# Sliding-window attention by key blocks, and projections of four tiles in two half passes

## The chip, the core and the metric

The kernel runs on one core of a Trainium2 chip. The core has five engines with their own instruction streams: PE (TensorE, matrix products into PSUM), DVE (VectorE), ACT (ScalarE), POOL (GpSimd) and SP (SyncE, which here issues DMAs). They wait for one another through semaphores. The metric is the device time of one execution in microseconds (us), as the median of several runs; a profiled execution gives the trace.

## The reference

Two layers of the same kind follow one another, with the same weights. Each adds an attention block and a block that changes a single row:

```python
def _A_ref(x, wqkv, wo):                      # S = 2048, D = 512
    H = 32; Dh = D // H; W = 256
    q, k, v = split(x @ wqkv)                 # 32 heads of 16
    scores = einsum("bhqd,bhkd->bhqk", q, k) * (Dh ** -0.5)
    mask = (i - j >= 0) & (i - j < W)
    p = softmax(where(mask, scores, -1e9))
    return einsum("bhqk,bhkd->bhqd", p, v) @ wo

def _B_ref(x, w_r, w_gate, w_up, w_down):     # F = 1792
    r = x @ w_r
    idx = argsort(-r)[:, :1]                  # the one row with the largest r
    y = (silu(x[idx] @ w_gate) * (x[idx] @ w_up)) @ w_down
    return x + scatter(y * sigmoid(r[idx]), idx)

x = A_x
x = x + _A_ref(layernorm(x)); x = x + _B_ref(layernorm(x))
x = x + _A_ref(layernorm(x)); x = x + _B_ref(layernorm(x))
```

Inputs and output are bf16.

## The kernel before

The 2,048 rows are 16 tiles of 128, so the two layers are 32 steps. The class Builder adds operations (engine, function, what it reads and writes, PSUM banks, an assumed duration, a priority) to a scheduler, Sched, which simulates them and fixes the order of each engine; a wait is put where an operand comes from another engine or a DMA. The priority is the step number plus a fraction, so that one step's work of several kinds is interleaved. Sched gives every engine a fixed order: an instruction that waits holds up all behind it.

**Projections** (proj, L546). The normalized tile XN (L521 on POOL, with 64 columns repeated at L523) is transposed by PE in sixteen half-height pieces (transposes, L525) into PSUM banks 6 and 7 (MISC), copied to XNT (evict_t, L544), and multiplied with the weights. The array is used as two row halves of 64, each with its own matmul and its own bank: in qk (L562) the upper half makes q and the lower k. For this the weights are stored split (load_split), and each half goes through all eight 64-row chunks; the repeated columns give each half the chunks that would lie in the other. The four column groups s (eight heads each) take 16 matmuls of 128 columns each, 64 for a tile. DVE copies k to KTN and q to QT (L569, L571). The v projection (L580) is 16 matmuls of 256 columns.

**Keys and values.** Keys are scattered into block-diagonal form, KBD, by eight DMAs on SP for a pair of tiles (kscat, L606); values go through DRAM (vd) into VBD (vscat, L616 and L622).

**Attention** (attention, L626). A step handles one query tile. For each of the four groups s there are three units (UNITS), which pack pieces of nine key blocks of 32 into 384 columns. A unit is up to eight score matmuls (L668), two matmuls that add the mask (L682), one exp on ACT over two banks (L689, 768 columns) into PT, and PV, 16 matmuls of 34 columns for every four blocks (L702). Units alternate between bank pairs 0/1 and 2/3; PV accumulates in banks 4 and 5. Then DVE takes the reciprocal of the denominators (L719) and normalizes (L724), and POOL repeats 64 columns (L726).

**Output projection** (out_proj, L728) transposes, multiplies (L742) and adds to the residual (L746), again in banks 6 and 7. mod_tile computes layernorm statistics and the router's value r on DVE and POOL.

**The one row.** After all 16 tiles of layer 0, select finds the row, through DRAM and gathers; mlp (L858) computes gate and up (L873, 56 matmuls each) and down (L888, 14) in bank 6, and later tiles get the row by a masked add (L509) from tile SKIP1 = 6 on, so the first six may be normalized before the row is known. In layer 1 the choice is made from NS2 = 13 tiles and its MLP is at the end of attention. If the row lies elsewhere, or a denominator is out of range, a flag starts a second, slower program (GBuilder) behind the first.

All of x lies in SBUF (XR, 16 tiles), and so do the three MLP weights, loaded once (L495 to L497). The steady order is set in build (L943): a step adds attention of tile T, output projection of T-1, and normalization and projection of T+3.

Of the kernel before, what the change touches and what calls it, by code (L numbers as in the profile page):

```python
# [8 lines left out]
F32 = mybir.dt.float32  # L9
BF16 = mybir.dt.bfloat16  # L10
I32 = mybir.dt.int32
ALU = mybir.AluOpType
# [44 lines left out]
class _Op:  # L57
    __slots__ = ("idx", "eng", "fn", "deps", "dur", "name", "is_dma", "prio", "signals", "count",
                 "dma_sem", "start", "end", "waits", "dma_extra")

    def __init__(self, idx, eng, fn, deps, dur, name, is_dma, prio):
# [14 lines left out]
        self.dma_extra = 0.0  # L76


class Sched:
# [64 lines left out]
    def needs_wait(self, op, dop):  # L144
        return dop.is_dma or dop.eng != op.eng or op.eng not in self.INORDER
# [175 lines left out]


UNITS = (
# [3 lines left out]
)  # L327
ACC = 4
MISC = 6
STEP = 1.0  # L330
NS2 = 13
SKIP1 = 6
DLO = 2.0 ** -60
DHI = 2.0 ** 60


class Builder:
# [16 lines left out]
    def alloc(self):  # L354
        nc = self.nc
        NT, SEQ, FF, NF = self.NT, self.SEQ, self.FF, self.NF
        self.RP = 3
        self.RQ = 6
        self.NU = 15
        self.XR = self.sb("XR", [128, NT, 516], F32)  # L360
        self.WQK = self.sb("WQK", [128, 8, 512], BF16)
        self.WV = self.sb("WV", [128, 8, 256], BF16)
        self.WO = self.sb("WO", [128, 8, 256], BF16)
        self.WG = self.sb("WG", [128, 4, FF], BF16)
        self.WU = self.sb("WU", [128, 4, FF], BF16)
        self.WD = self.sb("WD", [128, NF, 512], BF16)
        self.XN = self.sb("XN", [128, 2, 576], BF16)
        self.XNT = self.sb("XNT", [128, 2, 8, 128], BF16)
        self.QT = self.sb("QT", [128, self.RQ, 4, 128], BF16)
        self.KTN = self.sb("KTN", [128, 2, 2, 4, 128], BF16)  # L370
        self.KBD = self.sb("KBD", [128, self.RP, 2, 4, 4, 128], BF16)
        self.VN = self.sb("VN", [128, 2, 2, 4, 8, 17], BF16)
        self.VBD = self.sb("VBD", [128, self.RP, 8, 2, 8, 17], BF16)
        self.PT = self.sb("PT", [128, self.NU, 2, 512], BF16)
        self.ON = self.sb("ON", [128, 2, 576], BF16)
        self.OT = self.sb("OT", [128, 2, 8, 128], BF16)
        self.OUTB = self.sb("OUTB", [128, 2, 2, 512], BF16)
        self.JUNK = self.sb("JUNK", [128, 512], BF16)
        self.WR16 = self.sb("WR16", [128, 512], BF16)
        self.YBC = self.sb("YBC", [128, 512], F32)  # L380
        self.ONESB = self.sb("ONESB", [128, 128], BF16)
        self.ZEROB = self.sb("ZEROB", [128, 128], BF16)
# [40 lines left out]
    def xbf(self, m):  # L423
        return self.XR[:, m, 256:512].bitcast(BF16)

    def xin(self, L, m):
        return self.xbf(m) if L == 0 else self.XR[:, m, 0:512]
# [1544 lines left out]
```

## Time and profile before

| | us |
|---|---|
| median of 3 runs | 496.41 |
| lowest and highest | 495.53, 499.56 |
| profiled execution | 501.95 |
| its span, first to last instruction | 500.2 |

The profiled execution is 1.1% above the median. A row of the profile names the line, engine, operation, tile written and tiles read, and sizes. PEld is the loading of weights for a matmul. Slices are fortieths of the span. "issue" as the end of a wait means that nothing that the profile shows was waited for. A row of the stretches gives, for PE, PEld, DVE, ACT and POOL, the busy time and the number of instructions, then PE's granted clock and the DMA share and rate.

### The profile page before, as it was taken

What the parts mean: (1) busy time and instruction counts of PE and PEld (TensorE: products, weight loads), DVE (VectorE), ACT (ScalarE), POOL (GpSimd) and SP (SyncE); (2) the same over time, 40 slices, a digit from 0 to 9 for tenths busy, and PEclk for the clock granted to TensorE, in tenths of its full rate; (3) what the DMA queues carried; (4) which work ended last, traced back from release to release, by engine and by line L of the source; (5) the groups of instructions that cost most, each with busy time, mean ns of one, the idle gap of its engine ahead of it and who ended that gap; (6) DMA issues with size and microseconds to landing.
All of it is one profiled execution on the core that took longest, in us unless ns stands there. A gap on an engine that the chain in (4) does not pass through costs nothing.

```text
span 500.2 us, 29488 instructions
## 1 busy us (share of the span) xinstructions
PE 364.2 (73%) x13757; PEld 319.2 (64%) x13757; DVE 256.5 (51%) x558; ACT 274.4 (55%) x389; POOL 174.6 (35%) x438
## 2 busy tenths in 40 slices
PE   0168777887887787778787776777877787877860
PEld 0156767776776777777775654676776777766730
DVE  7663655555465554545567218765444555445242
ACT  0013467665676766666666620366666776787600
POOL 8721343233433443332324204644333332222012
PEclk9999999998999999999999567699999999998575
DMA  8982214131322222231323111232131404043000
GB/s 209 365 239 47 47 27 95 21 82 34 67 50 61 57 57 60 56 61 47 68 56 60 36 47 14 54 78 60 62 76 47 91 25 103 17 107 77 6 2 29
DMA packets 104808, 34.99 MB, mean 70 GB/s; under 512 B 87266, under 2 KB 100707, under 8 KB 104420
## 3 DMA queue, kind: packets, MB, share of 16 engines
q1 hardware_dynamic: 97428, 25.60, 22.4%
q10 hardware_dynamic: 7248, 7.41, 4.7%
q8 instruction: 110, 1.80, 1.5%
q14 instruction: 22, 0.18, 0.1%
HBM read 14.56 MB, written 14.22 MB: 58 GB/s over the span
## 4 chain that ended last, share of the span: by engine, by line
PE 57%; ACT 13%; issue 11%; DVE 8%; DMA 5%; ACTq 2%; POOL 1%; SPq 0%; DVEq 0%
ACT PT L689 13%; PE PS L562 12%; PE PS L668 12%; PE PS L702 12%; PE PS L742 6%; PE PS L580 6%; PE PS L536 3%; PE PS L682 2%; PE PS L888 2%; DMA WR<-in_B_w_r_dram 2%; ACTq L439 2%; DMA KBD<-KTN 1%; PE PS L873 1%; DVE VN L588 1%; DVE ON L724 1%
## 5 line engine op out<-in xcount | busy, mean ns | idle before, releaser
L689 ACT ACTIVATE PT<-PS 128x768 bf16<-128x768 f32 (+5 forms) x384 | 272.6, 772 | 164.7 <-PE PS L682 156.4
L668 PE MATMUL PS<-QT,KBD 64*128 64x128 bf16 (+3 forms) x2880 | 130.8, 208 | 41.3 <-ACT PT L689 26.8
L702 PE MATMUL PS<-VBD,PT 64*128 64x34 bf16 x5760 | 122.9, 176 | 23.5 <-issue 20.2
L702 PEld LDWEIGHTS PS<-VBD,PT 64*128 64x128 bf16 x5760 | 103.4, 94 | 29.4 <-issue 26.2
L668 PEld LDWEIGHTS PS<-QT,KBD 64*128 64x128 bf16 x2880 | 84.9, 96 | 57.5 <-ACT PT L689 36.9
L562 PE MATMUL PS<-XNT,WQK 64*128 64x128 bf16 x2048 | 73.7, 232 | 19.1 <-issue 9.8
L682 PE MATMUL PS<-BM,II 64*128 64x64 bf16 (+2 forms) x768 | 80.5, 200 | 1.2 <-issue 1.2
L562 PEld LDWEIGHTS PS<-XNT,WQK 64*128 64x128 bf16 x2048 | 66.6, 102 | 22.4 <-issue 17.3
L521 POOL TENSOR_SCALAR XN<-XR,RS 128x512 bf16<-128x512 bf16 (+1 forms) x32 | 24.5, 765 | 119.5 <-PE PS L536 106.9
L726 POOL COPY ON<-ON 128x64 bf16<-128x64 bf16 x32 | 7.9, 246 | 115.4 <-DVE ON L724 115.4
L569 DVE CAST KTN<-PS 128x512 bf16<-128x512 f32 x32 | 22.0, 688 | 47.2 <-PE PS L562 46.1
L746 DVE TENSOR_TENSOR XR<-PS,XR 128x512 f32<-128x512 f32 x32 | 22.1, 692 | 45.1 <-PE PS L742 43.8
L588 DVE CAST VN<-PS 128x512 bf16<-128x512 f32 x32 | 22.2, 693 | 39.7 <-PE PS L580 39.7
L682 PEld LDWEIGHTS PS<-BM,II 64*128 64x128 bf16 x768 | 42.0, 98 | 0.7 <-issue 0.7
L580 PE MATMUL PS<-WV,XNT 64*128 64x256 bf16 x512 | 36.8, 284 | 3.7 <-DVE QT L571 1.7
L742 PE MATMUL PS<-WO,OT 64*128 64x256 bf16 x512 | 35.9, 282 | 3.9 <-DVE OT L544 3.8
L544 DVE COPY OT<-PS 128x1024 bf16<-128x1024 bf16 x32 | 22.1, 689 | 27.4 <-PE PS L536 27.4
L536 PE MATMUL PS<-IDB,XN 64*128 64x64 bf16 x512 | 14.8, 196 | 24.1 <-POOL XN L523 17.2
L580 PEld LDWEIGHTS PS<-WV,XNT 64*128 64x128 bf16 x512 | 25.1, 99 | 7.6 <-DVE QT L571 2.6
L742 PEld LDWEIGHTS PS<-WO,OT 64*128 64x128 bf16 x512 | 24.5, 98 | 7.2 <-DVE OT L544 4.3
L536 PEld LDWEIGHTS PS<-IDB,XN 64*128 64x128 bf16 x512 | 10.4, 98 | 27.9 <-POOL XN L523 17.2
L724 DVE TENSOR_TENSOR ON<-PS,RD 128x256 bf16<-128x256 f32 x64 | 24.3, 418 | 0.8
(90 smaller groups left out, 363.3 us busy)
## 6 DMA issues: line engine op xcount, KB each, us to landing
scrx<-XR SPq DMA_DIRECT2D x14, 516.0 KB, 3.3
vd<-VN SPq DMA_DIRECT2D x15, 272.0 KB, 3.5
VBD<-vd SPq DMA_DIRECT2D x60, 68.0 KB, 2.5
KBD<-KTN SPq DMA_DIRECT2D x120, 32.0 KB, 3.2
XR<-in_A_x_dram SPq DMA_DIRECT2D x8, 256.0 KB, 8.9
WG<-in_B_w_gate_dram ACTq DMA_DIRECT2D x1, 1792.0 KB, 13.8
WU<-in_B_w_up_dram ACTq DMA_DIRECT2D x1, 1792.0 KB, 17.6
WD<-in_B_w_down_dram ACTq DMA_DIRECT2D x1, 1792.0 KB, 24.1
```

Of the source, the lines that this page charges most:

```text
L521: S.add("pool", lambda e: e.tensor_scalar(out=XN[:, k2, 0:512], in0=x, scalar1=RS[:, k4, 1:2], scalar2=RS[:, k4, 2:3], op0=ALU.mult, op1=A ...
L536: r = e.transpose(o, src[rows, idx, c:c + 128], self.IDB[rows, rows])
L544: S.add("dve", lambda e: e.tensor_copy(out=out, in_=src), banks=[MISC, MISC + 1], writes=[key], dur=620, name=name)
L562: r = e.matmul(self.PS[:, MISC + t, 128 * s:128 * s + 128], lhsT=self.WQK[rows, j, 128 * s:128 * s + 128], rhs=XNT[rows, k2, j, :], start= ...
L580: r = e.matmul(o, lhsT=XNT[rows, k2, j, :], rhs=self.WV[rows, j, :], start=(j == 0), stop=(j == 7))
L588: S.add("dve", lambda e: e.tensor_copy(out=vout, in_=vin), banks=[MISC, MISC + 1], writes=["vn%d_%d" % (pr % 2, m % 2)], dur=600, name="evv")
L668: r = e.matmul(self.PS[:, pair + x, c0:c0 + n], lhsT=self.KBD[rows, p3, tt, s, b4, :], rhs=self.QT[rows, q, s, q0:q0 + n], start=(bi == 0) ...
L682: r = e.matmul(o, lhsT=self.II[rows, :], rhs=w, start=False, stop=True, skip_group_check=True)
L689: return e.activation(out=self.PT[:, slot, :, off:off + ncols], in_=self.PS[:, pair:pair + 2, 0:ncols], func=ACTF.Exp, scale=0.25)
L702: r = e.matmul(acc[:, x, 34 * gg:34 * gg + 34], lhsT=self.PT[rows, slot, a, c:c + 128], rhs=self.VBD[rows, p3, 4 * tt + b4, :, gg, :], sta ...
L724: S.add("dve", lambda e, o=o, i0=i0, i1=i1: e.tensor_tensor(out=o, in0=i0, in1=i1, op=ALU.mult), reads=["rd%d_%d" % (L, t)], banks=[ACC + ...
L742: r = e.matmul(self.PS[:, MISC + x, 0:256], lhsT=self.OT[rows, k2, j, :], rhs=self.WO[rows, j, :], start=(j == 0), stop=(j == 7))
```

## The change

**Projections of four tiles.** Four tiles are normalized and transposed into one XNT of 512 columns (NBATCH = 4). The weights are stored plainly (WQKV), and eight transposes a tile are left. A projection has two passes: in the first the upper row half makes q (bank 6) and the lower k (bank 7), in the second they change places, so each output gets both halves of every 128-row chunk. The first matmul of the second pass waits until the first pass has been written (`force`, a wait of PE for itself). The v and the output projection are built alike. Matmuls of qk have 512 columns: 64 for four tiles.

**Key-major attention.** A step handles the four key blocks of one tile. Each block is scored for the 288 queries that can see it in one matmul a row half, masked at both ends by another, and exponentiated over 2 x 288 columns. PT keeps twelve key blocks, with zeroed edges, and the PV of query tile T takes the blocks of tiles T-2, T-1 and T, in three parts per group.

**Rest.** XR holds 12 tiles; layer 1 reads x back from DRAM (SCR). MLP weights come in six chunks of 896 KB on SP, through two buffers, in each layer (in layer 1 two chunks use the space of WQKV and XNT). Layer 0 chooses its row from NS1 = 11 tiles, its MLP is spread over the steps behind, and the row is corrected in DRAM before it is read back; the row must lie in tile 8 or later (SKIP1), and no later tile may have a larger value (late). In layer 1 NS2 is 12. The first batch scatters its keys on DVE, straight from PSUM, and is normalized on ACT; KBD has two buffers instead of three. The wrapped copies on POOL and the masked add are gone.

```diff
-NS2 = 13
-SKIP1 = 6
+NBATCH = 4
+NS1 = 11
+NS2 = 12
+SKIP1 = 8
+W = 288
+PITCH = 384
...
     def needs_wait(self, op, dop):
+        if op.force == dop.idx:
+            return True
...
-            for j in range(8):
-                c = 128 * j if j < 4 else 128 * (j - 4) + 64
+            for j in range(4):
                 for t in range(2):
...
+    def phases(self, fn, reads, dur, at, name, parts=1, gap=0.03, bank=MISC):
+        S = self.S
+        last = None
+        n = 4 // parts
+        for ph in range(2):
+            for k in range(parts):
+                js = range(n * k, n * k + n)
+                i = S.add("pe", lambda e, ph=ph, js=js: fn(e, ph, js), reads=reads, banks=[bank, bank + 1], dur=dur / parts, name=name,
+                          prio=at + gap * (parts * ph + k), extra_deps=[last] if last is not None else [])
+                if ph == 1 and k == 0:
+                    S.ops[i].force = last
+                last = i
+
+    def qk(self, b, s, at):
...
+        bank = (MISC, 0, 2, ACC)[s] if b == 0 else MISC
...
-                    r = e.matmul(self.PS[:, MISC + t, 128 * s:128 * s + 128], lhsT=self.WQK[rows, j, 128 * s:128 * s + 128],
-                                 rhs=XNT[rows, k2, j, :], start=(j == 0), stop=(j == 7))
+                    w = t ^ ph
+                    r = e.matmul(self.PS[:, bank + w, :], lhsT=self.WQKV[rows, j, 512 * w + 128 * s:512 * w + 128 * s + 128],
+                                 rhs=XNT[rows, kb, j, :], start=(ph == 0 and j == 0), stop=(ph == 1 and j == 3), skip_group_check=True)
...
         for s in range(4):
-            for u in range(3):
...
+            for b in range(4):
+                kb = 4 * t + b
+                n = min(W, self.SEQ - 32 * kb)
+                q0 = 32 * kb
...
+                        r = e.matmul(self.PS[:, pair + x, 0:n], lhsT=self.KBD[rows, k2, s, 4 * (T % 2) + b, :],
+                                     rhs=self.QT[rows, s, q0:q0 + n], start=True, stop=False, skip_group_check=True)
...
+                    o = self.PT[:, c0 - 96:c0 - 96 + 2 * PITCH].rearrange("p (a c) -> p a c", a=2)[:, :, 96:96 + n]
+                    return e.activation(out=o, in_=self.PS[:, pair:pair + 2, 0:n], func=ACTF.Exp, scale=0.25)
...
+            for part, (r0, r1) in enumerate(((-8, -4), (-4, 0), (0, 4))):
+                blocks = [4 * t + r for r in range(r0, r1) if 4 * t + r >= 0]
...
-            if T == NT + 1:
-                self.select(0, NT, at + 0.3)
...
-            g = T + 3
-            if g < NW:
-                lnp(g, at)
-                prj(g, at)
...
+            for L, n in ((0, NS1), (1, NS2)):
+                u = T - L * NT - n
+                if u == -2:
+                    self.load_mlp(0, at)
+                    self.load_mlp(1, at)
+                elif u == 0:
+                    self.select(L, n, at + 0.3)
+                elif u == 2:
+                    self.mlp_in(L, at - 0.6)
...
+                elif u == (5 if L == 0 else 4):
+                    self.mlp_down(L, 0, at - 0.4)
+                    self.mlp_down(L, 1, at - 0.2)
...
+            misc(T, at)
```

The order of PE in a steady step before, around the q/k projection of a tile. L668 and L682 are a score unit, L702 is PV, L562 the projection:

```order
L702 MATMUL PS<-VBD,PT 128x34 x16
L562 MATMUL PS<-XNT,WQK 128x128 x64
L668 MATMUL PS<-QT,KBD 128x64 x2
L668 MATMUL PS<-QT,KBD 128x128 x4
L668 MATMUL PS<-QT,KBD 128x64 x2
L682 MATMUL PS<-BM,II 128x2x2x32 x2
L668 MATMUL PS<-QT,KBD 128x96 x2
```

The order of PE in a steady step of the changed kernel, around the q/k projection of one group of four tiles (L584), its second pass behind the first; L682 and L688 are a score block, L716 is PV:

```order
L716 MATMUL PS<-VBD,PT 128x34 x32
L584 MATMUL PS<-XNT,WQKV 128x512 x8
L682 MATMUL PS<-QT,KBD 128x288 x2
L688 MATMUL PS<-BM,II 128x2x32 x2
L584 MATMUL PS<-XNT,WQKV 128x512 x8
L682 MATMUL PS<-QT,KBD 128x288 x2
L688 MATMUL PS<-BM,II 128x2x32 x2
L682 MATMUL PS<-QT,KBD 128x288 x2
L688 MATMUL PS<-BM,II 128x2x32 x2
L716 MATMUL PS<-VBD,PT 128x34 x48
```

64 matmuls in one run have become two runs of eight, with a score block of four matmuls between them.

The order of PE at the layer boundary before. XST is the chosen row, WG, WU and WD the MLP weights; L536 with L562 and L580 are projections of layer 1, L742 the output projection:

```order
L702 MATMUL PS<-VBD,PT 128x34 x16
L873 MATMUL PS<-XST,WG 128x1 x56
L873 MATMUL PS<-XST,WU 128x1 x56
L702 MATMUL PS<-VBD,PT 128x34 x32
L888 MATMUL PS<-WD,HT 128x512 x14
L536 MATMUL PS<-IDB,XN 128x64 x16
L562 MATMUL PS<-XNT,WQK 128x128 x64
L580 MATMUL PS<-WV,XNT 128x4x64 x16
L536 MATMUL PS<-IDB,ON 128x64 x16
L742 MATMUL PS<-WO,OT 128x256 x16
```

The order of PE around the first half of the gate and up products (L916, weights in MW) of layer 0 in the changed kernel, in tile 14:

```order
L682 MATMUL PS<-QT,KBD 128x256 x2
L688 MATMUL PS<-BM,II 128x32 x2
L716 MATMUL PS<-VBD,PT 128x34 x16
L916 MATMUL PS<-XST,MW 128x1 x56
L682 MATMUL PS<-QT,KBD 128x224 x2
L688 MATMUL PS<-BM,II 128x32 x2
L716 MATMUL PS<-VBD,PT 128x34 x16
L584 MATMUL PS<-XNT,WQKV 128x512 x8
L682 MATMUL PS<-QT,KBD 128x192 x2
```

The MLP products now stand among score blocks of layer 0, and the projections of layer 1 no longer stand behind them.

The order of PE at the end, before (L937 is the flag):

```order
L702 MATMUL PS<-VBD,PT 128x34 x48
L888 MATMUL PS<-WD,HT 128x512 x14
L536 MATMUL PS<-IDB,ON 128x64 x16
L742 MATMUL PS<-WO,OT 128x256 x16
L536 MATMUL PS<-IDB,ON 128x64 x16
L742 MATMUL PS<-WO,OT 128x256 x16
L937 MATMUL PS<-ONESB,BADB 1x1
```

And in the changed kernel (L954 is the down product, L1006 the flag):

```order
L716 MATMUL PS<-VBD,PT 128x34 x64
L546 MATMUL PS<-IDB,ON 128x64 x8
L750 MATMUL PS<-WO,OT 128x256 x16
L954 MATMUL PS<-MW,HT 1x512 x14
L1006 MATMUL PS<-ONESB,BADB 1x1
```

One output projection is left behind the last PV instead of two, and the down product has moved from ahead of it to behind it.

More of the change, by code (lines that the diff above doesn't have):

```diff
@@ L658, in loc @@
[L658 to L669 removed]
+                fr = (4 * s + b) / 16.0
@@ L707, in pv @@
[L707 to L716 removed]
+                                r = e.matmul(self.PS[:, ACC + x, 34 * gg:34 * gg + 34], lhsT=self.PT[rows, c:c + 128],
+                                             rhs=self.VBD[rows, v3, b8, :, gg, :], start=st, stop=last and kb == blocks[-1] and a == 1,
+                                             skip_group_check=True)
@@ L787, in mod_tile @@
[L787 to L800 removed]
+              reads=[sk], writes=[rk], dur=260)
```

754 lines of the change are left out of this document (404 added, 350 removed), and 3 rows, old and new, of the table UNITS.

## The prediction

> **What bounds the kernel now.** I read the page first, then the start times of one instruction that comes once per query tile, then the stretches, and last the waits of the matrix engine. In the page's busy table and slices, PE is the busiest engine at 73%, and ACT falls to nothing at three places: the first three slices, slices 25 and 26, and the last two.
>
> ```profile
> span 500.2 us, 29488 instructions
> PE 364.2 (73%) x13757; PEld 319.2 (64%) x13757; DVE 256.5 (51%) x558; ACT 274.4 (55%) x389; POOL 174.6 (35%) x438
> PE   0168777887887787778787776777877787877860
> ACT  0013467665676766666666620366666776787600
> q8 instruction: 110, 1.80, 1.5%
> ```
>
> The reciprocal of the denominators (L719) runs once at the end of each tile's attention, so its starts are the pace. The rows are the whole run, a stretch in the first layer, one in the second, and the pair around the layer boundary.
>
> ```profile
> L719 DVE RECIPROCAL RD<-PS x32: 347/353/358, 49.1 to 476.0; 128x32 f32<-128x32 f32 x32
> L719 DVE RECIPROCAL RD<-PS x11: 348/357/358, 120.0 to 249.2; 128x32 f32<-128x32 f32 x11
> L719 DVE RECIPROCAL RD<-PS x8: 347/348/358, 348.1 to 439.9; 128x32 f32<-128x32 f32 x8
> L719 DVE RECIPROCAL RD<-PS x2: 348/353/358, 294.8 to 334.6; 128x32 f32<-128x32 f32 x2
> ```
>
> So the span has four parts: 49.1 us until the first tile is done; a steady step of (249.2-120.0)/10 = 12.9 and (439.9-348.1)/7 = 13.1 us, 13.0 in all; one pair of tiles 39.8 us apart at the boundary; and 500.2-476.0 = 24.2 us behind the last tile.
>
> Within the steady step, PE is busy 15.66 of 20 us, which is 10.2 of 13.0, and ACT 14.41 of 20. What PE does in the rest is in the second and third row: each stretch holds exactly 128 weight loads and 128 matmuls, and begins behind a stop of PE for which nothing is waited for.
>
> ```profile
> 180.00:200.00 20.00, 15.66 (x668) 14.30 (x670) 9.47 (x19) 14.41 (x20) 7.79 (x21) 1.00 0.32 72
> 184.15:187.90 3.75, 2.63 (x128) 2.28 (x128) 1.81 (x4) 3.68 (x6) 1.73 (x3) 1.00 0.48 78
> 187.90:191.90 4.00, 3.14 (x128) 2.85 (x128) 2.65 (x6) 2.55 (x4) 1.36 (x2) 1.00 0.46 103
> PE PS L702 <- issue: 20.2, 29, 2.2
> PE PS L562 <- issue: 9.8, 12, 1.3
> PE PS L668 <- issue: 9.0, 15, 1.4
> PE PS L536 <- issue: 4.3, 7, 0.9
> PE PS L668 <- ACT PT L689: 26.8, 60, 1.0
> ```
>
> 256 instructions between stops, and 110 instruction packets on queue q8 for 2 x 13,757 = 27,514 of them (107 x 256): PE stops at each block of its own program. The four issue rows give 43.3 us in 63 stops, 0.69 us each. A step of 440 matmuls crosses 3.44 blocks, 2.4 us; 10.2 + 2.4 = 12.6 of the 13.0. PE bounds the steady step, and its number of instructions counts beside their columns.
>
> The Trainium skill, "Runtime: NRT & Kernel Launch", Instruction fetch mechanics, calls the price of crossing a 16 KiB boundary mostly hidden. The trace disagrees with 0.69 us per crossing; by the page the first term below would be nothing, and the sum some 18 us higher.
>
> **The step, part by part.** These rows carry the prices: groups in dense flow, and the exps by size.
>
> ```profile
> 192.31 1.96 PE L562 MATMUL PS<-XNT,WQK 64*128 64x128 bf16 x64
> 188.13 1.05 PE L742 MATMUL PS<-WO,OT 64*128 64x256 bf16 x16
> 181.07 0.61 PE L702 MATMUL PS<-VBD,PT 64*128 64x34 bf16 x32
> 186.02 0.37 PE L702 MATMUL PS<-VBD,PT 64*128 64x34 bf16 x16 [0.16 <-DVE ON L724]
> 183.73 4.50 ACT L689 ACTIVATE PT<-PS 128x768 bf16<-128x768 f32 x6 [0.43 <-PE PS L682]
> L689 ACT ACTIVATE PT<-PS 128x768 bf16<-128x768 f32 x336 | 251.6, 812 | 141.1 <-PE PS L682 139.7 <-PE PS L702 0.6
> L689 ACT ACTIVATE PT<-PS 128x576 bf16<-128x576 f32 x8 | 5.2, 649 | 1.5 <-PE PS L682 1.5
> L562 PE MATMUL PS<-XNT,WQK 64*128 64x128 bf16 x2048 | 73.7, 232 | 19.1 <-issue 9.8 <-DVE XNT L544 9.3
> ```
>
> - Instructions: per tile, qk 64 to 16, transposes 32 to 16, scores 96 to 32, mask 24 to 32; v projection, PV and output projection keep 16, 192 and 16. 440 become 320: 120/128 x 0.69 = -0.65 us.
> - Columns: qk had 64 x 128 and has 16 x 512; score blocks 1,152 columns a head group in both; mask 2,048 columns in both. At (1.96-0.23)/64 = 0.027 us per 128 columns that is no gain. Sixteen transposes fewer, at (0.61-0.37)/16 = 0.015 us each, are -0.24.
> - PV: eight of a tile's twelve key blocks come out of exps of the two tiles before, so only the last third can wait for this step's exps. PE waited 26.8 us for exps, 0.84 a step. I take half away, -0.4 (bounds 0 and -0.84).
> - Second halves: three projections a step (qk, v, out) wait for their first half to be written, because the row halves then swap banks. A score group stands between, so the wait may be nothing; bare, it is one matmul's 0.23. I take 0.07 each, +0.2 (0 to 0.7).
> - Exps: 12 of 768 become 16 of 576. Spacing is (4.50-0.81)/5 = 0.738 us, and 0.738-(0.812-0.649) = 0.575 for the small one: 16 x 0.575 = 9.2 against 8.9 a step. Covered as long as PE's step is longer; if it is not, this is the next floor.
> - DVE loses half of each transposed eviction and the row update, POOL two small copies: off PE's path, nothing.
>
> The step becomes 13.0-0.65-0.24-0.4+0.2 = 11.9 us.
>
> **Start, boundary, end, MLP.** The rows are: statistics of the first tiles, their normalization, the first q/k projection (twice as slow as later); the stretch at the boundary; the MLP products and the end; one load; one eviction.
>
> ```profile
> 11.95 1.22 DVE L512 BATCH_NORM_STATS2 ST<-XR 128x6 f32<-128x512 bf16 x2
> 15.45 1.52 POOL L521 TENSOR_SCALAR XN<-XR,RS 128x512 bf16<-128x512 bf16 x2
> 23.18 3.60 PE L562 MATMUL PS<-XNT,WQK 64*128 64x128 bf16 x64 [5.36 <-DVE XNT L544]
> 300.00:320.00 20.00, 13.48 (x234) 10.37 (x232) 15.07 (x30) 0.19 (x1) 10.40 (x26) 0.67 0.23 42
> 470.60 1.65 PE L873 MATMUL PS<-XST,WG 128*128 128x1 bf16 x56
> 475.87 4.51 PE L888 MATMUL PS<-WD,HT 128*128 128x512 bf16 x14
> 481.23 0.41 PE L536 MATMUL PS<-IDB,ON 64*128 64x64 bf16 x16 [0.85 <-DVE YBC L891]
> 484.39 0.41 PE L536 MATMUL PS<-IDB,ON 64*128 64x64 bf16 x16 [0.79 <-DVE XR L746]
> WD<-in_B_w_down_dram ACTq DMA_DIRECT2D x1, 1792.0 KB, 24.1
> L569 DVE CAST KTN<-PS 128x512 bf16<-128x512 f32 x32 | 22.0, 688 | 47.2 <-PE PS L562 46.1
> ```
>
> - Start: two tiles are normalized at 17.0; the next two follow 2 to 3 us later, since ACT now normalizes while POOL does only the statistics: four transposed tiles at 20.5. Then four tiles' q/k, one at 3.6 and three at 1.96 = 9.5, and 16 v matmuls, 1.0: first scores at 31. Sixteen exps 9.2 and the last PV, 1: the first tile is done at 41 (37 if statistics run ahead; 47 if POOL's memsets come first or PE stays slow).
> - Boundary: the choice for layer 0 is made from eleven tiles, five tiles early, and the chosen row is mended in DRAM. So the hole is gone; tile 16 follows tile 15 at PE's pace.
> - Light steps: 20 steps are full, 238 us. Tiles 1 and 17 have four key blocks fewer (64 matmuls at 0.015, half a block stop): 10.7 each. Tile 16 has eight fewer: 9.5. Tiles 14 and 15 have 320 and 832 of 1,152 score columns fewer in each of four head groups and two row halves, 0.5 and 1.4 us at 0.027 per 128: 11.4 and 10.5. Tiles 26 to 28 have no qk (16 x 0.108 = 1.8 less): 10.1 each; 29 no v projection either (1.0): 9.1; 30 and 31, with the score columns of 14 and 15, 8.6 and 7.7. With 238 + 21.4 + 9.5 + 21.9 + 30.3 + 25.4 that is 346.5.
> - MLP, formerly in the hole and at the end: gate and up are 2 x 1.65 a layer, the first layer's down 14 x 512 columns at 0.054 per 128 (no second row half beside it), 3.0, block stops 0.7 a layer: 7 + 4 = 11. Weights now come in chunks of 896 KB through two buffers, once a layer. The last of three loads of 1,792 KB landed 24.1 us after its issue, so 8 us for two chunks; the up chunks must land within most of a step behind the gate product: 3 us (0 to 8) of PE waiting.
> - End: 24.2 us, less what stood ahead of the last two output projections: the down product (475.87 to 481.23, of which 1.3 is still needed for normalizing) and a whole extra tile (481.23 to 484.39), 4.0 + 3.2. The down product now comes last and ends within the store's time. 17.0.
>
> Sum: 41 + 346.5 + 11 + 3 + 17 = 418.5. The profiled execution took 501.95 for a span of 500.2, so 420.3; the median shown, 496.41, is 0.989 of that execution: 416 us.
>
> **Rivals.** A step more or less counts some 28 times.
> - ACT becomes the bound. If the score groups, now one per key block with one small chunk of other work behind each, keep ACT fed, the step falls towards 9.2; with lumps of qk (8 x 0.108 = 0.86 us, longer than an exp) I put it at 10.2: 48 us less, 368. For it: nothing but scores waits for exps. Against it: PE's own 10.0 busy and 1.7 of stops exceed it.
> - The steady step gains nothing, because projections, transposes and evictions share PSUM banks 6 and 7 one after the other, as before. Only start, boundary and end gain: +1.1 x 28, 446.
> - Slower: that chain through banks 6 and 7 becomes the bound. Its links are 9.0 us a step, as before: transposes 0.41 twice, q/k 1.96, v and out 1.05 each, and six evictions of 0.69. A score group and its exp between the halves of three projections add 3 x 0.8; each eviction standing on average behind half another DVE instruction adds 6 x 0.35; block stops 1.7: 15.2, giving 507. It decides from a step of 15.0. Against it: PE's order puts other work into each gap.
> - The shortcut does not hold: layer 0 now accepts only rows 1024 to 1407 and layer 1 only rows below 1536, and otherwise a second, whole program runs behind: by an estimate as much again, some 850. On these inputs the router's largest values stand in rows 1105 and 1082.
>
> **How the numbers follow.** Forecast (step 11.3 to 12.5, start 37 to 47: 398 to 436) 0.52; ACT-bound 0.20; no steady gain 0.22; chain-bound 0.04; others 0.02. So 416, and 380 to 446 leaves out the last two and most of the ACT-bound case's faster half. A measurement can tell 1% from no change: faster 0.94, within 1% 0.02, slower 0.04.
>
> **What would show it.** Right: 79 or so instruction packets instead of 110; reciprocals 11 to 12.5 us apart; no ACT hole near the middle; first reciprocal near 41; less than 20 us behind the last. Wrong: reciprocals at 13 or more with DVE waiting for PE and PE for DVE on banks 6 and 7; PE stopping at weights (the MW tile) in tile 14; ACT over 90% busy in steady stretches, which would put the time below 380.

## The result, and the profile after

| | before | after |
|---|---|---|
| median of the runs, us | 497.99 (4 runs) | 434.86 (4 runs) |
| lowest and highest | 495.53, 501.46 | 433.31, 440.56 |
| profiled execution, us | 501.95 | 433.42 |
| its span, us | 500.2 | 431.7 |

The ratio of the times is 0.8718, with a 95% interval from 0.8633 to 0.8802: the changed kernel takes 12.8% less time. The ratio is one of mean times and leaves out the execution of 440.56 us, which at 1.7% above the fastest counts as slow. The time lies inside the predicted range and 19 us above the predicted 416.

The page of the changed kernel, the same lines as before:

```profile
span 431.7 us, 22240 instructions
PE 354.1 (82%) x10109; PEld 246.1 (57%) x10109; DVE 227.5 (53%) x551; ACT 295.8 (69%) x526; POOL 152.5 (35%) x373
PE   0598898799899999698699978899999998739862
ACT  2257788778988898765285858777988788845400
PEclk9999999899999999989569999989999999956555
q8 instruction: 81, 1.33, 1.3%
```

ACT no longer falls to nothing at the layer boundary; its lowest slice there is the twentieth, at 2 tenths. Two places are left where PE's clock falls for long: slices 20 and 21 (205 to 227 us), with PE less busy in the first, and the last five (from 378 us).

The starts of the reciprocal (now L729), tile by tile stretches of the changed kernel:

```profile
L729 DVE RECIPROCAL RD<-PS x32: 340/357/359, 44.3 to 411.1; 128x32 f32<-128x32 f32 x32
L729 DVE RECIPROCAL RD<-PS x11: 347/348/359, 64.2 to 177.2; 128x32 f32<-128x32 f32 x11
L729 DVE RECIPROCAL RD<-PS x7: 347/357/359, 177.2 to 258.3; 128x32 f32<-128x32 f32 x7
L729 DVE RECIPROCAL RD<-PS x11: 340/358/359, 258.3 to 370.4; 128x32 f32<-128x32 f32 x11
L729 DVE RECIPROCAL RD<-PS x4: 351/358/358, 370.4 to 411.1; 128x32 f32<-128x32 f32 x4
```

The steady step of the first layer is (177.2-64.2)/10 = 11.3 us. Set against the terms of the prediction, with its MLP terms put where they fall (10 us in tiles 13 to 18, 4 in tiles 29 to 31):

| stretch | predicted | measured | difference |
|---|---|---|---|
| until tile 0 is done | 41.0 | 44.3 | +3.3 |
| tiles 1 to 12 | 141.6 | 132.9 | -8.7 |
| tiles 13 to 18 | 75.9 | 81.1 | +5.2 |
| tiles 19 to 28 | 113.6 | 112.1 | -1.5 |
| tiles 29 to 31 | 29.4 | 40.7 | +11.3 |
| behind the last reciprocal | 17.0 | 20.6 | +3.6 |
| span | 418.5 | 431.7 | +13.2 |

That the span came so near is in part luck: stretches off by -10.2 us in sum stand against stretches off by +23.4.

The other 5.7 us of the 18.9 lie between span and median: the prediction took off 1.1%, since the profiled execution of before was that much slower than its median, and here the two agree.

What PE waited for in ten steady steps, in the kernel before (120.0 to 249.2 us):

```profile
PE PS L668 <- ACT PT L689: 11.2, 23, 1.0
PE PS L702 <- issue: 6.1, 10, 1.1
PE PS L562 <- issue: 3.8, 5, 1.1
PE PS L668 <- issue: 2.7, 5, 1.0
PE PS L536 <- issue: 0.6, 1, 0.6
```

And in ten of the changed kernel (64.2 to 177.2 us):

```profile
PE PS L546 <- DVE KTN L605: 3.3, 3, 1.8
PE PS L682 <- ACT PT L696: 2.7, 13, 0.4
PE PS L716 <- issue: 0.9, 2, 0.5
PE PS L682 <- issue: 0.9, 1, 0.9
```

The stops at program blocks fell from 13.2 us in 21 to 1.8 in 3, far more than the number of blocks did (110 to 81 packets). The waits for exps fell from 11.2 to 2.7. New is a wait of 3.3 us behind the eviction of k.

The late stretch is explained by the sequence of the changed kernel around tile 29, where the maxima of the router are exchanged through DRAM (vcd, BC):

```profile
369.43 0.63 SPq L883 DMA_DIRECT2D WQKV<-in_B_w_up_dram  x1
370.10 0.64 SPq L883 DMA_DIRECT2D XNT<-in_B_w_up_dram  x1
...
372.90 0.57 SPq L834 DMA_DIRECT2D vcd<-VC  x1
...
384.28 0.34 SPq L835 DMA_DIRECT2D BC<-vcd  x1
...
387.49 0.29 DVE L837 TENSOR_REDUCE MT<-BC 128x1 f32<-128x128 f32 x1 [11.63 <-DMA BC<-vcd]
387.81 0.20 ACT L846 ACTIVATE MT<-MT 128x1 f32<-128x1 f32 x1 [6.35 <-DVE MT L837]
...
388.50 0.32 PE L682 MATMUL PS<-QT,KBD 64*128 64x160 bf16 x2 [4.74 <-ACT PT L696]
```

A store of 1 KB, issued at 372.90 behind two loads of 896 KB, had landed at 384.28, when its read-back was issued. DVE waited 11.6 us for what followed; ACT's next instruction was an exp on the result, so the attention's exps stood behind it, and PE behind them.

### The profile page after: what moved, and what is told of

It is laid out like the page before. It is cut to its first block, busy times and chain, and to the rows that moved or that the text cites. A ratio compares the mean times of both kernels' runs of the same rounds, so it can differ in the third digit from the quotient of the medians.

```text
span 431.7 us, 22240 instructions
## 1 busy us (share of the span) xinstructions
PE 354.1 (82%) x10109; PEld 246.1 (57%) x10109; DVE 227.5 (53%) x551; ACT 295.8 (69%) x526; POOL 152.5 (35%) x373
## 4 chain that ended last, share of the span: by engine, by line
PE 53%; ACT 15%; DMA 10%; DVE 7%; SPq 6%; issue 5%; POOL 3%; DVEq 0%; ACTq 0%; POOLq 0%
ACT PT L696 14%; PE PS L584 13%; PE PS L682 11%; PE PS L716 9%; PE PS L750 7%; PE PS L620 6%; DMA vcd<-VC 4%; SPq L639 4%; PE PS L954 2%; DVE XR L755 2%; PE PS L688 2%; DMA KBD<-KTN 2%; DMA BC<-vcd 2%; PE PS L546 2%; PE PS L916 1%
## 5 line engine op out<-in xcount | busy, mean ns | idle before, releaser
L696 ACT ACTIVATE PT<-PS 128x576 bf16<-128x576 f32 (+5 forms) x512 | 287.0, 621 | 85.8 <-PE PS L688 82.4
L682 PE MATMUL PS<-QT,KBD 64*128 64x288 bf16 (+6 forms) x1024 | 146.6, 291 | 27.9 <-ACT PT L696 17.8
L716 PE MATMUL PS<-VBD,PT 64*128 64x34 bf16 x5760 | 116.2, 176 | 7.1 <-issue 4.4
L716 PEld LDWEIGHTS PS<-VBD,PT 64*128 64x128 bf16 x5760 | 97.5, 94 | 18.4 <-issue 10.2
L688 PE MATMUL PS<-BM,II 64*128 64x64 bf16 (+1 forms) x1024 | 100.5, 194 | 2.7 <-issue 2.7
L682 PEld LDWEIGHTS PS<-QT,KBD 64*128 64x128 bf16 x1024 | 52.0, 96 | 66.0 <-ACT PT L696 40.5
L584 PE MATMUL PS<-XNT,WQKV 64*128 64x512 bf16 x512 | 69.3, 396 | 3.3 <-DVE VN L627 2.2
L688 PEld LDWEIGHTS PS<-BM,II 64*128 64x128 bf16 x1024 | 52.4, 98 | 9.3 <-issue 2.2
L603 DVE CAST QT<-PS 128x512 bf16<-128x512 f32 x28 | 19.4, 692 | 48.5 <-PE PS L584 48.5
L620 PE MATMUL PS<-WQKV,XNT 64*128 64x256 bf16 x512 | 40.4, 277 | 2.2 <-DVE XR L755 1.6
L584 PEld LDWEIGHTS PS<-XNT,WQKV 64*128 64x128 bf16 x512 | 22.0, 97 | 26.3 <-issue 4.2
L627 DVE CAST VN<-PS 128x512 bf16<-128x512 f32 x32 | 22.1, 692 | 15.3 <-PE PS L620 12.5
L750 PEld LDWEIGHTS PS<-WO,OT 64*128 64x128 bf16 x512 | 21.9, 102 | 11.4 <-DVE OT L554 2.6
L620 PEld LDWEIGHTS PS<-WQKV,XNT 64*128 64x128 bf16 x512 | 20.9, 95 | 10.7 <-DVE XR L755 3.4
L529 POOL TENSOR_SCALAR XN<-XR,RS 128x512 bf16<-128x512 f32 (+1 forms) x28 | 21.5, 769 | 10.1 <-PE PS L546 9.4
```

What stands on the lines that cost most here:

```text
L529: S.add("pool", lambda e: e.tensor_scalar(out=XN[:, k2, :], in0=x, scalar1=RS[:, k4, 1:2], scalar2=RS[:, k4, 2:3], op0=ALU.mult, op1=ALU.add),
L584: r = e.matmul(self.PS[:, bank + w, :], lhsT=self.WQKV[rows, j, 512 * w + 128 * s:512 * w + 128 * s + 128], rhs=XNT[rows, kb, j, :], start ...
L603: S.add("dve", lambda e: e.tensor_copy(out=self.QT[:, s, tok], in_=self.PS[:, MISC, :]), banks=[MISC], writes=["qt%d_%d" % (b % 4, s)], du ...
L620: r = e.matmul(o, lhsT=XNT[rows, kb, j, 128 * jt:128 * jt + 128], rhs=self.WQKV[rows, j, 1024 + 256 * w:1280 + 256 * w], start=(ph == 0 an ...
L627: S.add("dve", lambda e: e.tensor_copy(out=vout, in_=vin), banks=[MISC, MISC + 1], writes=["vn%d_%d" % (pr % 2, m2)], dur=650, name="evv")
L682: r = e.matmul(self.PS[:, pair + x, 0:n], lhsT=self.KBD[rows, k2, s, 4 * (T % 2) + b, :], rhs=self.QT[rows, s, q0:q0 + n], start=True, sto ...
```

## The experiments

The kernel before was run beside each, on chips where it took 502.6 to 505.8 us (medians), so the ratio to it counts, not the microseconds; of kernels run once, the steps of the trace count. "Tiles 13 to 18" is the time between the reciprocals of tiles 12 and 18, and so on.

**e1, the loads behind the exchange.**

```diff
-self.load_mlp(2, at + 0.5, (self.WQKV...))
-self.load_mlp(3, at + 0.5, (self.XNT...))
+self.load_mlp(2, at + 0.5, (self.WQKV...), ["vcd1"])    # reads: wait for the store
+self.load_mlp(3, at + 0.5, (self.XNT...), ["vcd1"])
```

> Only the two loads of the up weights in layer 1 (into WQKV and XNT) are moved, behind the store and the read-back by which the router's maxima are exchanged (vcd, BC). Theory A: in the changed kernel that 1 KB store landed 11.4 us after its issue because 1,792 KB stood ahead of it in the same queue; DVE waited 11.6 us for BC, ACT 6.4, PE 5.0, so the step of tile 29 took 17.9 us. Then DVE's wait falls under 5 us, tile 29 takes 10 to 12 us and the whole 425 to 430 us. Rival B: the same delay comes back as PE waiting for the up weights, which now come later: tile 29 gets shorter, tile 30 (13.4) longer by as much, and the whole stays within 2 us of 434.9.

Waits of this kernel from 360 to 395 us:

```profile
DVE MT L837 <- DMA BC<-vcd: 4.9, 1, 4.9
PE PS L682 <- ACT PT L696: 3.2, 12, 0.8
```

Tile 29 took 11.2 us instead of 17.9, tiles 30 and 31 together 24.6 instead of 22.9. Median 431.03, ratio 0.8588 (0.8509 to 0.8667). So theory A holds for the place, though its total of 425 to 430 us was missed, and a quarter of the 6.7 us gained in tile 29 came back in tiles 30 and 31, as B had it. The interval overlaps that of the changed kernel; the step shows the effect better than the total.

**e4, loads an eighth in size.**

```diff
-e.dma_start(dst, src)
+m = dst.shape[2] // 8
+e.dma_start(dst[:, :, 0:m], src[:, :, 0:m])
```

> Left out: seven eighths of every MLP weight load (each chunk's DMA fetches an eighth of its columns, the buffers are zeroed once early), so the MLP's values are not the reference's; every instruction stays. Theory A (the loads' traffic makes the steps around the MLP long, through late small DMAs and late program blocks): tiles 13 to 18, 81.1 us in the changed kernel, fall to about 70, the stops of PE without a visible cause between 200 and 216 us (1.1, 0.6 and 3.0 us) fall under 0.7 each, and tile 29 falls from 17.9 to about 12; the whole 415 to 420 us. Rival C (the MLP's one-column matmuls and the waits around them halve PE's clock, whatever the loads do): tiles 13 to 18 stay above 77 us, with the clock at 0.5 for some 17 us in tiles 15 and 16; only tile 29 gets shorter, the whole about 427.

Tiles 13 to 18 took 74.4 us instead of 81.1, tile 29 11.9, the tail 18.7, the span 421.8. PE's stops without a visible cause between 180 and 232 us: 1.2 at most. In tiles 13 to 18 the clock was at 0.5 for single stretches of 3.4 us only. So the traffic of the weights costs about 7 us in tiles 13 to 18, and rival C falls; in e1, e3, e6 and e8, with whole loads, these tiles took 82.0 to 82.7. Theory A's 70 was not reached either. Tiles 1 to 12, which have no such traffic, took 137.5 instead of 132.9 here. PE had more to do in them, 3,760 weight loads and 123.4 us instead of 3,732 and 119.8: the planner simulates the shorter loads and ordered PE's work anew from 33 us on, and part of what the changed kernel does ahead of tile 0's end came later. Tiles 13 to 18 hold as many matmuls in both kernels (1,832). Single tiles differ by 2 to 3 us from trace to trace (tile 23 took 10.5 us in the changed kernel and 13.0 in e1, which does not touch it).

**e8, the loads on another queue.**

```diff
-self.S.dma("sp", lambda e: e.dma_start(dst, src), writes=keys, ...
+self.S.dma("act", lambda e: e.dma_start(dst, src), writes=keys, ...
```

> All loads of MLP weights are issued by ACT instead of SP, at the same places of the plan; bytes and sizes stay. Theory A1 (what delays the router's exchange is the order within one queue): the 1 KB store lands in under 4 us, tile 29 takes 11 to 13 us instead of 17.9, while tiles 13 to 18 stay at 79 to 83, since PE's program blocks still come late beside the traffic. Rival A2 (it is the traffic itself, at 0.9 to 1.0 of the DMA engines, whatever the queue): the store still takes over 8 us and tile 29 over 15.

The DMAs of this kernel from 355 to 400 us, with KB and us to landing:

```profile
WQKV<-in_B_w_up_dram ACTq DMA_DIRECT2D x1, 896.0 KB, 7.1
XNT<-in_B_w_up_dram ACTq DMA_DIRECT2D x1, 896.0 KB, 12.6
...
vcd<-VC SPq DMA_DIRECT2D x1, 1.0 KB, 10.9
```

The store took 10.9 us, with no load in its queue; tile 29 took 16.0 us. Three stores of 1,044 KB in all stood ahead of it, as they did in e1, where it had landed 4.3 us after its issue (375.17 to 379.44). It is the traffic of the loads (A2), not their place in the same queue (A1). So e1 helped because the bytes came later, not because the store stood ahead of them in the queue.

**e9, the loads in four pieces.**

```diff
-S.dma("sp", ... e.dma_start(dst, src), ..., prio=at)
+for q in range(4):
+    S.dma("sp", ... e.dma_start(dst[:, :, q*m:q*m+m], src[:, :, q*m:q*m+m]), ..., prio=at + 0.2 * q)
```

> Each chunk of 896 KB is loaded by four DMAs of 224 KB, planned a fifth of a step apart; same bytes. Theory J (bursts: a program block that is asked for while 1.8 MB are under way waits for them): the longest stop of PE without a visible cause between 200 and 230 us, 3.0 us in the changed kernel and 3.8 to 4.0 in two of its variants, falls under 1.5 and tiles 13 to 18 from 81.1 to 76 to 78 us. Rival K: the pieces are issued one behind the other as soon as the buffer is free, so the traffic is as dense as before; the stop stays over 2.5 us and tiles 13 to 18 over 80.

The longest stop without a visible cause between 200 and 230 us was 1.4, as J had it, yet tiles 13 to 18 took 88.1 us. Waits of PE and DVE from 186 to 262 us:

```profile
DVE KTN L605 <- DMA KBD<-KTN: 6.3, 1, 6.3
PE PS L716 <- DMA VBD<-vd: 5.6, 2, 3.4
```

The scatters of keys and values, which SP issues between the pieces, now came late: DVE waited 6.3 us for one of the keys, PE 3.4 for one of the values. Theory J has the stops right; for the total neither theory holds.

**e3 and e10, the wait for KTN.** e3 only moved the projections; e10 gave the half of KTN that is scattered last a second buffer.

```diff
 # e3
-((0.6, 0.25, 0.85, 0.5) if b else
+((0.95, 0.4, 0.9, 0.5) if b else
 # e10
-self.KTN = self.sb("KTN", [128, 2, 4, 256], BF16)
+self.KTN = self.sb("KTN", [128, 3, 4, 256], BF16)
...
-out=self.KTN[:, :, s, :], in_=kps
+out=self.KTN[:, 0:2 + b % 2:1 + b % 2, s, :], in_=kps
```

> Only the places of the first three q/k projections of a batch move (0.95, 0.4 and 0.9 of a step instead of 0.6, 0.25 and 0.85). Theory H: in the changed kernel DVE waited 10.8 us, five times, with the eviction of k (KTN, L605) until the DMAs that scatter the batch before had read KTN, and PE's transposes waited 4.7 us for that eviction; later, the scatter is done first: DVE's wait falls under 4 us, PE's under 2, and the whole falls by 3 to 5 us. Rival I: PE meets the same work a little later and waits there instead (for DVE, or for exps); the whole stays within 2 us.

> The second half of KTN, which is scattered last, gets two buffers, so that the next batch's k need not wait for that scatter (the room comes from letting the updated row share the tiles of the router's choice). The run with later q/k projections had left DVE's wait at 11.9 us, so it had not tried this. Theory H: DVE's wait for the scatter (10.8 us, five times) and PE's wait behind it (4.7 us) vanish, and the whole falls by 4 to 6 us, ratio to the kernel before 0.855 to 0.865. Rival I: the next thing in banks 6 and 7 or the exps take the place of the wait; the ratio stays within 0.005 of 0.872.

The same wait in the changed kernel, in e3 and (what is left of it, on PE's weight loads) in e10:

```profile
DVE KTN L605 <- DMA KBD<-KTN: 10.8, 5, 3.6
```

```profile
DVE KTN L605 <- DMA KBD<-KTN: 11.9, 5, 3.3
```

```profile
PEld PS L547 <- DVE KTN L606: 0.9, 5, 0.2
```

e3 did not take the wait away (span 433.1) and so says nothing of its price. e10 did: span 427.7, median 430.49, ratio 0.8588 (0.8532 to 0.8645), that is 4 us by the spans and 1.5% by the ratios, whose intervals just overlap. Theory H has the total right. The place does not bear it out: tiles 1 to 18, with the ten steady steps of the first layer among them, hold the same work in both kernels and took 215.6 us instead of 214.0 in the profiled executions (c3 and c4 below, with the same buffer, 217.8). In those ten steps (63.5 to 180.6 us) exps took the wait's place, as rival I had it, 6.0 us instead of 2.7:

```profile
PE PS L684 <- ACT PT L698: 6.0, 24, 0.4
```

The gain lies in tiles 19 to 28 (109.3 instead of 112.1), the tail (19.0 instead of 20.6) and 0.7 us or less elsewhere. So what the wait by itself costs is not shown.

**e5, scores in thirds.**

```diff
-r = e.matmul(self.PS[:, pair + x, 0:n], ..., rhs=self.QT[rows, s, q0:q0 + n], start=True, ...)
+for c in range(0, n, 96):
+    m = min(96, n - c)
+    r = e.matmul(self.PS[:, pair + x, c:c + m], ..., rhs=self.QT[rows, s, q0 + c:q0 + c + m], start=(c == 0), ...)
```

> Each score matmul of 288 columns is split into three of 96 on the same columns: 64 matmuls a step more, 384 instead of 320. Theory D: PE's stops at its program blocks are gone from the steady step of the changed kernel because a block now lasts longer than its successor's fetch, some 2.5 us from the start of the fetch to the first instruction used; with 384 matmuls a step the last 70 matmuls of a block take about 2 us again, stops of 0.3 to 0.6 us come back at most blocks, three a step, and the steady step of the first layer goes from 11.1 to 12.5 to 13.5 us. Rival E: the stops went away for another reason (where in the order they fall, fewer waits); then only the fixed cost of 64 small matmuls is added, some 0.6 us, the step is 11.5 to 12 and stops over 0.3 us stay rare.

Ten steps of this kernel, their starts (its line 731 is the reciprocal) and what PE waited for in them:

```profile
L731 DVE RECIPROCAL RD<-PS x11: 345/356/358, 66.0 to 190.4; 128x32 f32<-128x32 f32 x11
```

```profile
PE PS L718 <- issue: 7.4, 7, 2.3
PE PS L684 <- ACT PT L698: 2.5, 11, 0.4
PE PS L684 <- issue: 1.6, 1, 1.6
```

The step went from 11.3 to 12.4 us and the span to 457.5. Stops came back: 9.7 us in ten steps (with two of 0.4 and 0.3) instead of 1.8. That is 0.8 a step more, as theory D had it, though the stops are fewer and less even than it said and the step just misses its 12.5; waits for KTN fell by 0.2. PE's busy time, in the stretches below, rose from 101.8 to 108.05 us, 0.6 a step, which looks like rival E's fixed cost of 64 small matmuls. It is not: the output projection, which the edit leaves alone, took longer too (e5 first, then the changed kernel):

```profile
L752 PE MATMUL PS<-WO,OT 64*128 64x256 bf16 x160 | 16.3, 336 | 0.4 <-DVE OT L554 0.2
L750 PE MATMUL PS<-WO,OT 64*128 64x256 bf16 x160 | 13.0, 285 | 0.4 <-DVE OT L554 0.2
```

PE's clock was halved for 19.4 us of these ten steps, with PE busy for 19.1 of them, against 3.4 in the changed kernel. If half clock doubles PE's time (half of the down product took 3.15 us at half clock and 1.67 at full, below), that is by an estimate 9.5 us against 1.7, more than the whole rise. In stretches at full clock alone, three matmuls of 96 columns took 0.145 us of PE and one of 288 took 0.141 (17.7/122 from 130.0 to 174.4 us in e5, 36.9/262 from 87.3 to 177.2 in the changed kernel). So E's fixed cost is not seen, and the stops came with a second cost, the halved clock: each halved stretch followed one of fewer than 6,700 columns, the upper end of theory L's band (e11, below). The three stretches, of before, of the changed kernel and of e5:

```profile
120.00:249.20 129.20, 103.07 (x4379) 93.63 (x4375) 65.00 (x135) 88.90 (x121) 47.83 (x121) 1.00 0.25 56
```

```profile
64.20:177.20 113.00, 101.80 (x3184) 73.27 (x3184) 61.24 (x145) 94.37 (x162) 40.87 (x100) 0.98 0.35 84
```

```profile
66.00:190.40 124.40, 108.05 (x3829) 86.50 (x3820) 61.21 (x145) 94.84 (x162) 39.43 (x98) 0.92 0.32 75
```

**e6, the down product of layer 1 earlier.**

```diff
-elif u == (5 if L == 0 else 4):
+elif u == 3 and L == 1:
+    self.mlp_down(L, 0, at + 0.3)
+    self.mlp_down(L, 1, at + 0.5)
```

> In layer 1 the down product and its two row updates stand in the step of tile 31 instead of behind the last output projection. Theory F: the 20.6 us behind the last reciprocal (17.0 were predicted) are set by the down product, 2 x 3.2 us at half clock with its row updates and stops, as the last on PE; moved ahead, the tail falls to 12 to 14 us, tile 31 grows by 3 to 4, and the whole falls by 3 to 5 us to about 431. Rival G: the tail is set by the last output projection, its statistics and the store, so it stays above 18 and tile 31 gets longer: 436 to 439 us.

Tail 15.3 us instead of 20.6, tile 31 12.9 instead of 9.5: 2 us in sum; median 435.66, ratio 0.8669 (0.8606 to 0.8732), which the totals alone don't tell from the changed kernel. Theory F has the sign right and the size too large. The two halves of the product in this kernel ran for the most part at half clock, and at full clock:

```profile
412.67 2.96 PE L954 MATMUL PS<-MW,HT 128*1 128x512 bf16 x7
...
416.56 1.67 PE L954 MATMUL PS<-MW,HT 128*1 128x512 bf16 x7
```

**e11, more columns in the light tiles.**

```diff
+for x in range(2 if n < W else 0):
+    r = e.matmul(self.PS[:, pair + x, 0:W], ..., rhs=self.QT[rows, s, self.SEQ - W:self.SEQ], start=True, ...)
 for x in range(2):
```

> In tiles 14 and 15 of each layer, whose score blocks have fewer than 288 columns, each block gets two more matmuls of 288 columns, whose results are overwritten: 4,608 columns per tile and row half more, about 2 us a tile at full clock. Theory L: PE's granted clock is halved for a stretch of 3.41 us whenever fewer than some 6,200 columns (of 64 rows; 16,000 would be possible) were streamed in the stretch before; so in the traces so far, without exception over some 850 stretches but for a band from 5,700 to 6,700. With the added columns tiles 14 and 15 have 1.0 in most stretches from 200 to 225 us and from 385 to 410 us (before: 0.5 for 17 us, and from 377 to the end but for 3.4 us), and tiles 30 and 31 take no longer than the 22.9 us of the changed kernel, in spite of 4 us more of work. Rival M: the clock follows the stops and waits of PE, not its columns; the low stretches stay, and tiles 14, 15, 30 and 31 take 6 to 12 us more.

Ratio 0.873 (0.8681 to 0.8778). Tiles 14 and 15 took 30.0 us instead of 25.9, tiles 30 and 31 24.7 instead of 22.9, so the added work did not pay, against L's end, and the 5.9 us in sum come close to the 6 that rival M had at its least. The clock, however, followed the columns. From 200 to 225 us it was halved for 9.6 us instead of 17, as L had it; from 385 to 410 us it still was for 17.2 instead of 21.6. Stretches of 3.41 us of the changed kernel:

```profile
203.30:206.70 3.40, 2.47 (x107) 2.17 (x101) 2.01 (x5) 1.60 (x6) 1.02 (x4) 1.00 0.35 45
206.70:210.20 3.50, 3.05 (x91) 2.80 (x89) 1.02 (x5) 0.61 (x2) 2.25 (x7) 0.51 0.55 139
210.20:213.60 3.40, 2.07 (x79) 1.85 (x75) 1.12 (x2) 1.10 (x4) 1.06 (x2) 0.50 0.96 298
...
217.00:220.40 3.40, 3.27 (x64) 1.75 (x60) 2.21 (x7) 3.20 (x6) 0.57 (x1) 0.50 0.40 49
220.40:223.80 3.40, 3.14 (x34) 1.98 (x36) 0.79 (x2) 2.38 (x5) 0.00 (x0) 0.50 0.45 71
223.80:227.20 3.40, 2.98 (x58) 1.81 (x58) 3.16 (x9) 3.05 (x6) 1.74 (x4) 1.00 0.28 46
```

Counted from the matmuls' records, columns of 64 rows started in a stretch (a column of 128 rows counts twice) and the clock in the next one:

| changed kernel: start, columns | next clock | e11: start, columns | next clock |
|---|---|---|---|
| 203.3: 4,950 | 0.5 | 205.1: 8,644 | 1.0 |
| 206.7: 4,922 | 0.5 | 208.6: 5,132 | 0.5 |
| 210.2: 3,840 | 0.5 | 212.0: 7,904 | 1.0 |
| 213.6: 3,648 | 0.5 | 215.4: 5,308 | 0.5 |
| 217.0: 5,600 | 0.5 | 218.8: 2,532 | 0.5 |
| 220.4: 7,424 | 1.0 | 222.2: 6,080 | 0.5 |

Rival M falls as to the clock: PE was busy for 3.27 of 3.40 us at 217.0 and the clock stayed low.

**c2, c4 and c3, edits together.** c2 joins e1, e3, e6 and e9; c4 joins e1, e6, e10 and a later load of the gate weights of layer 1; c3 is c4 without that.

```diff
 # c4 only
-self.load_mlp(0, at)
-self.load_mlp(1, at)
+r = ["rd6"] if L == 1 else []
+self.load_mlp(0, at, reads=r)
+self.load_mlp(1, at, reads=r)
```

> Four edits together: the layer-1 loads of the up weights behind the router's exchange, loads in four pieces, the q/k projections later, the down product of layer 1 in tile 31. If their gains add (5 to 7, 3 to 5, 3 to 5 and 3 to 5 us of 434.9), the ratio to the kernel before is 0.835 to 0.85 and the profiled run 415 to 421 us; if they only uncover one another, 425 to 430 us.

> Loads of the up weights in layer 1 behind the router's exchange, the down product of layer 1 in tile 31, the second buffer for half of KTN, and the gate weights of layer 1 not before tile 22 (in the changed kernel they come at tiles 16 and 17, with the read-back of x). The loads stay whole. If the gains add: tile 29 at 11 to 12 us, the tail at 15 to 16, no wait for KTN, tiles 17 and 18 together 26 instead of 28.4: 413 to 420 us in the profiled run, ratio 0.83 to 0.85. If they only uncover other waits, the ratio is 0.855 to 0.865.

> As the four-edit kernel before it, but with the gate weights of layer 1 loaded where the changed kernel loads them: there, moved to tile 22, the same burst cost 5.3 us as a stop of PE in tile 23 (16.8 us). Theory: KTN's wait gone (4 us less, as measured), tile 29 at 11 to 12 us (6 less), the tail at 15.5 with tile 31 at 13 (1 to 2 less in sum): 419 to 423 us of span and a ratio of 0.835 to 0.85 to the kernel before. Rival: what one edit frees, the bursts of weights in tiles 14 to 17 and the halved clock take back, and the ratio stays at 0.855 to 0.86.

| | ratio | span | tiles 1 to 12 | 13 to 18 | 19 to 28 | 29 to 31 | tail |
|---|---|---|---|---|---|---|---|
| changed kernel | 0.8718 (0.8633 to 0.8802) | 431.7 | 132.9 | 81.1 | 112.1 | 40.7 | 20.6 |
| c2 | 0.8673 (0.8566 to 0.8780) | 437.4 | 134.0 | 86.7 | 115.7 | 33.1 | 24.2 |
| c4 | 0.8564 (0.8523 to 0.8606) | 430.4 | 138.3 | 79.5 | 113.8 | 39.4 | 15.6 |
| c3 | 0.8448 (0.8390 to 0.8506) | 425.6 | 137.6 | 80.2 | 108.6 | 38.6 | 16.2 |

c2 gained nothing that can be told from the changed kernel, which is neither of its two cases: the pieces cost what they did in e9, and the planner put the down product ahead of the last output projection but behind its tile, so the tail grew. In c4, whose ratio is that of its second case, the gate weights' burst only moved: tile 23 took 16.8 us, with a stop of 5.3. c3 is the fastest version: 15.5% under the kernel before, its interval clear of the changed kernel's. Its ratio lies where the sum of the gains had put it, its span 2.6 us above. In its tiles 1 to 18 nothing was gained: 217.8 us instead of 214.0. PE's longest waits from 186 to 262 us are stops beside the loads of up and down weights:

```profile
PE PS L718 <- issue: 5.2, 1, 5.2
...
PE PS L690 <- issue: 3.8, 1, 3.8
```

## Why the prediction was right, and where it was off

**The steady step** (11.9 predicted, 11.3 measured): the mechanism was right, two sizes were too small. "120/128 x 0.69 = -0.65" priced a block's stop as fixed, so only their number would fall. It also charged 0.69 us to every crossing (2.4 us a step), though its own 63 stops stand against 107 blocks; in the ten steps shown above, stops took 1.3 us a step and waits for exps 1.1. Idle time of PE's matmuls at stops fell by (13.2-1.8)/10 = 1.1 us a step, because most stops vanished. The records of the instruction queue show why: in both kernels the next block's packet starts about 75 (50 to 100) matmuls before the block ends, and where PE stopped, its first matmul started 2.2 to 3.1 us after the packet. By an estimate from the stretches above, 75 matmuls last 2.2 us in the kernel before (75 x 129.2/4,379), 2.7 in the changed one (75 x 113.0/3,184) and 2.4 in e5 (75 x 124.4/3,829), which brought stops back. So the longer matmuls let most blocks arrive in time; the lead was not varied by itself. The prediction cited the Trainium skill, "Runtime: NRT & Kernel Launch", Instruction fetch mechanics, that a crossing is mostly hidden: the changed kernel's steady step agrees with that (0.18 us a step), the kernel before (1.3) doesn't.

**Exps** (-0.4 predicted): (11.2-2.7)/10 = -0.85, the lower bound. **Transposes** (-0.24): their two groups took 8.6 us of PE in the ten steps before and 6.1 in those of the changed kernel, -0.25 a step, as priced; that PE's whole busy time fell only from 10.3 to 10.2 is in part the 3.4 us at half clock. **Second halves** (+0.2): no such wait among the steady rows; nothing. **Missing:** the wait behind KTN, 0.33 a step; e10 took it away, but does not show what it costs. It was readable from the code, one KTN for a batch whose second half is scattered at the last moment.

**MLP weights, 3 us (0 to 8):** the size was too small and the mechanism another: about 7 us in tiles 13 to 18, inside the bounds, and 10 us of the whole span by e4 (421.8), outside them. PE never waited for a chunk. The traffic delays other things: the router's exchange (e1, e8), PE's program blocks, the scatters. Without it tiles 13 to 18 take 74.4 us (predicted 75.9, with the 3 us in it, so 72.9), so the terms of layer 0's MLP and of the light tiles were right to 1.5 us in sum. How the 7 us divide between late blocks (a stop of about 3 to 5.3 us stood there in every kernel with whole loads, against 1.2 in e4 and 1.4 in e9), half clock and late DMAs stays open.

**Tiles 29 to 31 (+11.3)** are the step that failed. The prediction had layer 1's selection of the row cost nothing in the steady order; no term stood for the wait that DVE and ACT, both in order, take on for it. e1 showed 6.7 us of it in tile 29 and 4.9 in sum. Beside the rest stands the halved clock, which held from 377 us to the end but for one stretch, while the prediction priced these tiles at full clock; no run raised the clock there without adding work, so its share is not shown.

**The tail** (17.0 predicted, 20.6): "The down product now comes last and ends within the store's time" was wrong. In the trace it is the last on PE, 3.15 and 3.14 us at half clock with a row update behind each, and the store of tile 31 is issued (420.34) before its second half starts (420.67); without it the tail is 15.3 (e6). **The start** (41 predicted, 44.3): scoring began at 27.7, earlier than the 31 assumed, but tile 0 then took 16.6 us. Groups of PE in these (27.7 to 44.4 us):

```profile
L584 PE MATMUL PS<-XNT,WQKV 64*128 64x512 bf16 x34 | 4.5, 378 | 0.5 <-DVE VN L627 0.5
...
L620 PE MATMUL PS<-WQKV,XNT 64*128 64x256 bf16 x48 | 3.6, 270 | 0.1
```

Projections (L584, L620) took 8.1 us of PE between the scores; no run tried this.

**Rivals.** ACT was busy for 94.37 of 113.00 us in the steady stretch, so it is no bound at 11.3. The step fell, so "no steady gain" and the chain through banks 6 and 7 are out; the latter shows only in the wait for KTN. The shortcut held. Of the signs, packets (81) and steps agree; the first reciprocal and the tail don't. The time lies just inside the forecast's own 398 to 436, with the step at its fast end and the rest slow, which is not the way that the forecast had it.

## What to carry to other kernels

Bulk loads that nothing waits for are not free: give short DMA round trips, on which an in-order engine waits, a time when no bulk load is under way, and read the cost in stops and scatters, not in waits for the loaded tile. Fewer and longer matmuls gain twice when PE stops at program blocks: fewer blocks, and blocks long enough to hide the next one's arrival. In e5 stops also cost clock: the time that PE stood still kept the columns of a stretch low. Taking a wait away (the second buffer of e10) is not yet a gain: read, stretch by stretch, what takes its place.

## What was not expected of the hardware

- A store of 1 KB took 11.4 us to land beside 1,792 KB of loads in its own queue, and 10.9 beside the same loads in another; without them, 4.3.
- PE's granted clock changed only at steps of 3.41 us in these traces, and it went with the columns of the stretch before. In 1,669 stretches of the 14 traces of this study (from 25 us on): below 5,100 columns of 64 rows the next stretch was at half clock in 194 of 194, above 6,700 in 0 of 1,341; 134 lay between. The fullest stretch had 15,744. Some matmul records are missing, which may widen the band. The Trainium skill, "TensorE: Matmul & The Clock Gate", HAM oscillation, warns of idle gaps of PE over 3.4 us; here it fell after a stretch in which PE was busy for 2.47 of 3.40 us and stayed low after one with 3.27 (4,950 and 5,600 columns), and the measurement decides.
- At half clock the down product of 7 x 512 columns took 3.15 us, at full clock 1.67.
